# Twelve of the 72 weight pieces rounded between the blocks of the experts

## The chip, the cores and the metric

The kernel runs on one core of one Trainium2 chip. The metric is the device time of one execution in microseconds (us). The kernel before has three timed runs: 1114.82, 1117.33 and 1116.95 us, so a median of 1116.95 us.

## The reference, cut to what matters

```python
def _attn_ref(q, k, v):                       # 4 batches, 12 heads, 448 tokens, 64 wide
    scores = scale * np.matmul(q, k.transpose(0, 1, 3, 2)) - np.log(S)
    return np.matmul(1.0 / (1.0 + np.exp(-scores)), v)

def _moe_ref(x, expert_emb, tau, w1, w2):     # 1792 tokens of 768; 8 experts, 1024 wide
    expert_idx = np.argmax(logits, axis=1)
    for e in range(E):
        mask = expert_idx == e
        h = np.maximum(x[mask] @ w1[e], 0.0)
        out[mask] = gate_w[mask, None] * (h @ w2[e])

def _moe2_ref(x, w_a, w_b, w_out):            # 768 -> 1536 -> 768, weights in float64
    return ((x @ w_a) * (x @ w_b) @ w_out).astype(np.float32)
```

The three parts run one after the other: the attention's output is what the experts route, and their output is what the last part multiplies. `w_a`, `w_b` and `w_out` reach the kernel as float64, and no engine computes in that type.

## The kernel before, in words

**Pieces and units.** The last part's 1536 columns are cut into twelve steps `f` of 128. The weights of a step are three tiles (`w_a`, `w_b`, `w_out`) of 128 partitions by 768, and each tile is handled in two halves, so there are 72 units. `prep_load` (L171) fetches a unit's raw 64-bit words, 384 KB, into one of four `raw` buffers. `prep_unit` (L185) turns them into float32 with integer arithmetic: two instructions on VectorE (L195, L197, into one of two or three buffers `m`), two on ScalarE (L199, and L201 into one of three buffers `ab`) and one addition on GpSimd (L202). `prep_finish` (L205) makes the last instruction on VectorE (L212), and with `behind=1` leaves the newest unit for a later call, so that its addition has time. `prep_store` (L221) writes the result to a scratch tensor `wm` in DRAM. `prep_tick` (L226) is one round of all four, for one unit: store what is finished, finish what is added, fetch the unit three further on, start the next one.

**When units are done before.** `F_EARLY = 4` puts the 24 units of steps 0 to 3 into the attention, one `prep_tick` for each pair of heads and three extra ones. Their results pass through `wm`. The other 48 units belong to the last part's first group of rows.

**The experts.** The tokens of each half of the batches are sorted by expert into blocks of 128, and `block1` (L852) does one block `b`: transpose and split the next block's tokens, two halves of the first product (`p1`, 18 matmuls each), a transpose of the hidden rows (`h_tr`, split into `hTh` and `hTl`), the second product (`p2`, 48 matmuls), the scaling by the gate on VectorE (`y`), and a scatter of `y` by GpSimd. All matmuls work on float32 numbers split into a high and a low half: ScalarE makes the high half (L728), VectorE subtracts it to get the low one (L729). Where the next block has another expert, the new `w1` (six tiles, 1024 wide) and `w2` (eight, 768 wide) are split inside `tc.If` blocks: `w1` while the second product runs, `w2` around the start of the next block. Such a block is called a changing block below. The first 14 blocks (`LIVE`) always run, later ones only if they hold tokens. `tick()` inside a block pumps the routing work that is left and issues none of the rounding.

**The last part.** Rows are taken in four groups (512, 512, 512 and 256 rows), each of twelve steps. Step `i` splits the weights of step `i+1` (`w_split`), multiplies (`ab`: 36 matmuls on PE into two PSUM buffers; ScalarE copies the first half out, L1040, VectorE multiplies the second by it, L1043), transposes rows of the next group in steps 4 to 11 (`y_tr`, L724), and adds the step before into the output (`out_mm`, 24 matmuls). From step 4 on, `y_tr` sits between the two PSUM buffers, so the next step's first matmul takes the buffer that L1043 has to release. In the first group, `prep_more` does rounding units between these pieces, four in an even step and five in an odd one, as far as step `i+5`. Units of a step in this group are written straight into the buffer that `w_split` reads, and `w_split` calls `prep_tick` itself where the six units it needs are not yet finished. `w_load` (L982) fetches a step's weights from `wm` where they were not rounded in place. Every transfer named here is issued in program order by SP's one queue; every engine also works in program order.

Of the kernel before, what the change touches and what calls it, by code (L numbers as in the profile page):

```python
# [24 lines left out]
def build(ctx: ExitStack, tc: tile.TileContext, q, k, v, emb, tau, w1, w2, wa, wb, wo, out, dbg=None, stop=None):  # L25
# [27 lines left out]
    LIVE = LIVE0 + -(-CAP[1] // P)  # L53
# [107 lines left out]

    HU = DM // 2
    units = [(f, part, hf) for f in range(NF) for part in range(3) for hf in range(2)]
    F_EARLY = 4
    next_unit, unit_end = [0], [6 * F_EARLY]
    prep_raw = {}

# [53 lines left out]
    def prep_store(dma=nc.sync):  # L221
        while prep_out:
            o, t = prep_out.pop(0)
            dma.dma_start(out=o, in_=t)

    def prep_tick(dma=nc.sync, behind=0):  # L226
        prep_store(dma)
        prep_finish(behind)
        prep_load(next_unit[0] + 3, dma)
        prep_unit()  # L230
# [507 lines left out]
    def load_w(which, expert, pair):  # L738
        t, src = (r1[pair], w1) if which == 1 else (r2[0][:, 2 * pair:2 * pair + 2, :], w2)
        nc.sync.dma_start(out=t, in_=src[expert, 2 * pair * P:2 * (pair + 1) * P, :].rearrange("(k p) c -> p k c", p=P))  # L740

    def split_w(which, kk, pool=None):
        hi, lo = (w1h, w1l) if which == 1 else (w2_t["h"], w2_t["l"])
        t = r1[kk // 2][:, kk % 2, :] if which == 1 else r2[0][:, kk, :]
        split(hi[kk], lo[kk], t, hi[kk].bitcast(F32))
# [97 lines left out]
    def moe(r2_p):  # L843
        pool = moe_pool
        w2h, w2l, hTh, hTl = w2_t["h"], w2_t["l"], hT["h"], hT["l"]
        mx_p = pool("mx", 2)
        r2.append(r2_p.tile([P, KF, DM], F32, name="r2"))
        ps_1 = pool("ps_1", 2, space=PSUM)
        ps_2 = pool("ps_2", 2, space=PSUM)
        ps_x = pool("ps_x", 4, space=PSUM)  # L850
        misc["ps"] = lambda: ps_x.tile([P, 512], F32, tag="px", name="px")
        def block1(b, chg, was_new, load, e_load):  # L852
            def when_new(fn, chg=chg):
                if chg is not None:
                    with tc.If(chg == 1):
                        fn()

            def load_new(which):
                for i in range((KD if which == 1 else KF) // 2):
                    load_w(which, e_load, i)  # L860

            def split_new(which, k0, k1):
                for kk in range(k0, k1):
                    split_w(which, kk)

            def p1(hf, inner):
                p1_half(b, hf, ps_1.tile([P, FH], F32, tag="p1", name="p1"),
                        mx_p.tile([P, FH], F32, tag="h", name="h"), inner)

            def p2(yp, k0, k1):  # L870
                for kk in range(k0, k1):
                    for l, wv in ((hTh, w2h), (hTh, w2l), (hTl, w2h)):
                        for hf in range(2):
                            nc.tensor.matmul(yp[hf][:, :HD], lhsT=l[:, kk, :], rhs=wv[kk][:, hf * HD:(hf + 1) * HD],  # L874
                                             start=kk == 0 and wv is w2h and l is hTh,
                                             stop=kk == KF - 1 and l is hTl)

            def tick():
                if b < LIVE:
                    pump()  # L880
                    pump()

            if b > 0:
                when_new(lambda: load_new(1), load)
                p1(0, lambda: None)
                when_new(lambda: split_new(2, KF // 2, KF - 2), was_new)
                tick()

                def rest():
                    h_tr(b, 0)  # L890
                    when_new(lambda: split_new(2, KF - 2, KF), was_new)

                p1(1, rest)
                tick()
                when_new(lambda: load_new(2), load)
            yp = [ps_2.tile([P, 512], F32, tag="p2", name="p2") for _ in range(2)]
            p2(yp, 0, 1)
            h_tr(b, 1)
            p2(yp, 1, 2)
            x_load(b + 1)  # L900
            if b == 0:
                split_new(2, 4, KF)
                when_new(lambda: load_new(1), load)
                when_new(lambda: load_new(2), load)
            when_new(lambda: split_new(1, 0, KD))
            p2(yp, 2, KF // 2)
            gather(b + 2)
            tick()
            p2(yp, KF // 2, KF)
            tick()  # L910
            y = mx_p.tile([P, DM], F32, tag="y", name="y", bufs=1)
            for hf in range(2):
                nc.vector.tensor_scalar(out=y[:, hf * HD:(hf + 1) * HD], in0=yp[hf][:, :HD],
                                        scalar1=slots[:, 2, b:b + 1], scalar2=None, op0=ALU.mult)
            when_new(lambda: split_new(2, 0, KF // 2))
            ph = 0 if b < LIVE0 else 1
            j = b - TB[ph][0]

            nc.gpsimd.indirect_dma_start(out=ys_d if b < LIVE else ys_d[:Y0, :], out_offset=bass.IndirectOffsetOnAxis(ap=idy[ph][:, j:j + 1], axis=0),
                                         in_=y, in_offset=None)  # L920

        for i in range(2, KF // 2):
            load_w(2, e_of[0], i)

        def block(b, was_new=None):
            nx = b + 1
            if nx < NBLK:
                if b + 2 >= LIVE0:
                    while bg:
                        pump()  # L930
                chg = value(nx, 1, 1, [ET.Activation, ET.DVE, ET.Pool])
                load = value(b + 2, 3, 1, [ET.SP])
                e_load = value(b + 2, 4, E - 1, [ET.SP])
                live = value(nx, 0, 1, ENGINES) if nx >= LIVE else None
            else:
                chg = load = e_load = None
            block1(b, chg, was_new, load, e_load)
            if nx == LIVE:
                first_loads()
            if nx < LIVE:  # L940
                block(nx, chg)
            elif nx < NBLK:
                with tc.If(live == 1):
                    block(nx, chg)

        block(0)
        moe_s.close()


    def glu():  # L950
# [31 lines left out]
        def w_load(i):  # L982

            if i < len(steps):
                t = w_raw(i)
                if F_EARLY <= i < NF:
                    wraw[i] = [(s, slice(0, DM), t[:, s, :]) for s in range(3)]
# [7 lines left out]
        def w_split(i, parts=range(3), eng=nc.vector):  # L995
            if i < len(steps):
                if parts[0] == 0:
                    wsp[i] = [ws_p.tile([P, 3, DM], F32R, tag=nm, name=nm) for nm in ("whi", "wlo")]
                while F_EARLY <= i < NF and wr_n.get(i, 0) < 6:
                    prep_tick()  # L1000
# [170 lines left out]
```

## Time and profile before

| | |
|---|---|
| timed runs, median | 1116.95 us |
| the profiled execution | 1113.61 us, its span 1111.9 us |
| PE busy | 1070.6 us (96%) |
| VectorE busy | 603.3 us (54%) |
| ScalarE busy | 500.3 us (45%) |
| GpSimd busy | 178.2 us (16%) |
| DMA | 182.98 MB, mean 165 GB/s |
| 20th to 28th of 40 slices, PE in tenths | 9 9 7 9 8 8 8 9 8 |

The span runs through attention (up to about 205 us), the experts (up to about 546 us) and the last part. PE is busy in nearly every slice, and the slices that are below 9 lie in the change from attention to the experts, at the end of the experts and in the first group of the last part. A share over the whole span says little here, since the three parts have different limits; the rows below are therefore of single stretches. Times in rows are from the span's start.

### The profile page before, as it was taken

The page shows a single profiled execution, that of the slowest core. Times are in us where ns is not written, and L with a number is a line of the kernel's source. Part 1 is how long each engine was busy: PE and PEld are TensorE (multiplying, and loading weights), DVE is VectorE, ACT ScalarE, POOL GpSimd, SP SyncE. Part 2 cuts the span into 40 slices and gives each one's busy share as a digit, 9 for nine tenths or more (in the row PEclk, how much of TensorE's full clock was granted, in tenths as well). Part 3 has the DMA queues.
Part 4 walks back from the last instruction along what each step waited for, and adds up shares of the span by engine and source line. Part 5 has one row for each costly group of instructions (what it writes and reads, how often), then busy time and mean ns, then how long its engine had stood idle before and what let it go on. Part 6 is the DMA issues. An engine that isn't in the chain of part 4 may idle for free.

```text
span 1111.9 us, 16742 instructions
## 1 busy us (share of the span) xinstructions
PE 1070.6 (96%) x5996; PEld 870.6 (78%) x5996; DVE 603.3 (54%) x1037; ACT 500.3 (45%) x761; POOL 178.2 (16%) x218
## 2 busy tenths in 40 slices
PE   7999999999999999999798889899999999999998
PEld 4555555599989898989787677788888888888997
DVE  2556688864853585352287998643333343333553
ACT  5766767431743474431355556333323232223442
POOL 2121322231221222121123343200000000000000
PEclk9999999999999999999899999999999999999999
DMA  9478586436644775331368566545231072220730
GB/s 201 138 199 214 150 231 197 165 106 266 230 185 169 270 263 192 136 136 45 106 216 278 173 211 214 198 155 214 91 122 43 4 295 103 110 86 1 310 131 29
DMA packets 108681, 182.98 MB, mean 165 GB/s; under 512 B 49560, under 2 KB 80792, under 8 KB 102560
## 3 DMA queue, kind: packets, MB, share of 16 engines
q1 hardware_dynamic: 104608, 166.54, 44.7%
q0 software_dynamic: 3040, 14.94, 3.8%
q8 instruction: 49, 0.80, 0.3%
q14 instruction: 56, 0.46, 0.1%
q10 hardware_dynamic: 928, 0.23, 0.1%
HBM read 149.45 MB, written 32.24 MB: 163 GB/s over the span
## 4 chain that ended last, share of the span: by engine, by line
PE 36%; DVE 9%; DMA 3%; issue 2%; ACT 1%; POOLq 0%; POOL 0%; SPq 0%; ACTq 0%; DVEq 0%
PE ab L1035 8%; PE ab L1037 8%; PE ab L1036 8%; PE o L1068 4%; PE o L1069 4%; PE o L1070 4%; DVE wlo L729 3%; DVE m L195 2%; DVE m L197 1%; DVE wx L212 1%; DMA r<-wm 1%; DMA yg<-ys 1%; DVE r L212 1%; DVE m L1043 1%; DVE gl L729 0%
## 5 line engine op out<-in xcount | busy, mean ns | idle before, releaser
L1035 PE MATMUL ab<-yh,whi 128*128 128x512 f32 (+1 forms) x576 | 211.8, 368 | 17.1 <-DVE m L1043 13.8
L1036 PE MATMUL ab<-yl,whi 128*128 128x512 f32 (+1 forms) x576 | 210.7, 366 | 0.0
L1037 PE MATMUL ab<-yh,wlo 128*128 128x512 f32 (+1 forms) x576 | 210.4, 365 | 0.0
L1035 PEld LDWEIGHTS ab<-yh,whi 128*128 128x128 f32 x576 | 109.7, 190 | 35.2 <-DVE m L1043 15.3
L1037 PEld LDWEIGHTS ab<-yh,wlo 128*128 128x128 f32 x576 | 109.7, 190 | 17.7 <-DVE wlo L729 0.2
L1036 PEld LDWEIGHTS ab<-yl,whi 128*128 128x128 f32 x576 | 109.6, 190 | 16.0
L202 POOL TENSOR_TENSOR m<-m,raw 128x384 int32<-128x384 int32 x72 | 81.8, 1136 | 240.9 <-DVE m L197 77.8
L1068 PE MATMUL o<-whi,gh 128*128 128x512 f32 x336 | 114.7, 341 | 0.0
L1069 PE MATMUL o<-whi,gl 128*128 128x512 f32 x336 | 113.8, 339 | 0.0
L1070 PE MATMUL o<-wlo,gh 128*128 128x512 f32 x336 | 112.9, 336 | 0.0
L536 ACT ACTIVATE a<-ps,bias_s 112x896 f32<-112x896 f32 x96 | 91.6, 1005 | 30.6 <-PE ps L535 30.2
L728 ACT CAST gh<-m 128x512 fp32r<-128x512 f32 (+1 forms) x48 | 27.2, 567 | 169.5 <-DVE m L1043 169.5
L1043 DVE TENSOR_TENSOR m<-ab,a 128x512 f32<-128x512 f32 (+1 forms) x48 | 29.9, 623 | 128.3 <-PE ab L1037 128.3
L729 DVE TENSOR_TENSOR wlo<-r,whi 128x768 fp32r<-128x768 f32 x70 | 65.7, 993 | 45.8 <-ACT whi L728 45.8
L729 DVE TENSOR_TENSOR wlo<-wx,whi 128x768 fp32r<-128x768 f32 x72 | 67.5, 992 | 42.5 <-ACT whi L728 42.5
L790 PE MATMUL p<-w1h,xl 128*128 128x512 f32 x216 | 85.3, 395 | 2.4 <-DVE xl L729 2.4
L788 PE MATMUL p<-w1h,xh 128*128 128x512 f32 x216 | 86.6, 401 | 0.1
L789 PE MATMUL p<-w1l,xh 128*128 128x512 f32 x216 | 84.6, 392 | 0.0
L547 PE MATMUL av<-a,v 112*64 112x448 f32 x384 | 82.5, 551 | 0.0
L874 PE MATMUL p<-w2h,hTh 128*128 128x384 f32 x288 | 76.3, 345 | 0.0
L791 ACT ACTIVATE h<-p 128x512 f32<-128x512 f32 x34 | 20.4, 599 | 123.8 <-PE p L790 123.8
L728 ACT CAST whi<-wx 128x768 fp32r<-128x768 f32 x72 | 55.6, 832 | 42.1 <-PE o L1069 30.2
(224 smaller groups left out, 1894.5 us busy)
## 6 DMA issues: line engine op xcount, KB each, us to landing
wx<-wm SPq DMA_DIRECT2D x20, 1152.0 KB, 9.4
r<-wm SPq DMA_DIRECT2D x19, 1152.0 KB, 6.0
r<-in_moe_w_dram SPq DMA_DIRECT2D x28, 768.0 KB, 8.6
r<-in_moe_w_dram SPq DMA_DIRECT2D x18, 1024.0 KB, 6.3
raw<-in_moe_w_a_dram SPq DMA_DIRECT2D x24, 384.0 KB, 3.4
raw<-in_moe_w_b_dram SPq DMA_DIRECT2D x24, 384.0 KB, 3.5
raw<-in_moe_w_out_dram SPq DMA_DIRECT2D x24, 384.0 KB, 5.4
q<-in_q_dram SPq DMA_DIRECT2D x48, 112.0 KB, 4.3
```

Of the source, the lines that this page charges most:

```text
L536: nc.scalar.activation(out=a[:, c2], in_=ps[:, :, :S], func=AF.Sigmoid, bias=bias_s[:CP], scale=qscale)
L728: nc.scalar.copy(out=hi, in_=src)
L729: eng.tensor_tensor(out=lo, in0=src, in1=f32_hi, op=ALU.subtract)
L788: nc.tensor.matmul(ps, lhsT=xh[:, kk, :], rhs=w1h[kk][:, cs], start=kk == 0, stop=False)
L789: nc.tensor.matmul(ps, lhsT=xh[:, kk, :], rhs=w1l[kk][:, cs], start=False, stop=False)
L790: nc.tensor.matmul(ps, lhsT=xl[:, kk, :], rhs=w1h[kk][:, cs], start=False, stop=kk == KD - 1)
L1035: nc.tensor.matmul(ps[:, :n], lhsT=hi[:, s, cs], rhs=yh[:, kk, :n], start=kk == 0, stop=False)
L1036: nc.tensor.matmul(ps[:, :n], lhsT=hi[:, s, cs], rhs=yl[:, kk, :n], start=False, stop=False)
L1037: nc.tensor.matmul(ps[:, :n], lhsT=lo[:, s, cs], rhs=yh[:, kk, :n], start=False, stop=kk == KD - 1)
L1068: nc.tensor.matmul(t[:, d0:d1], lhsT=gh[:, cs], rhs=hi[:, 2, d0:d1], start=first, stop=False)
L1069: nc.tensor.matmul(t[:, d0:d1], lhsT=gl[:, cs], rhs=hi[:, 2, d0:d1], start=False, stop=False)
L1070: nc.tensor.matmul(t[:, d0:d1], lhsT=gh[:, cs], rhs=lo[:, 2, d0:d1], start=False, stop=last)
```

## The change

```diff
-    F_EARLY = 4
+    F_EARLY = 6
...
             p2(yp, 2, KF // 2)
             gather(b + 2)
             tick()
+            if 0 < b < LIVE - 1:
+                prep_tick(behind=1)
             p2(yp, KF // 2, KF)
             tick()
```

`F_EARLY = 6` makes the units of steps 4 and 5 early ones too. The attention still has 24 ticks, so it fetches three units more and rounds as many as before. Blocks 1 to 12 of the experts each round one unit, and 36 are left for the first group. The weights of steps 4 and 5 now pass through `wm`, so `w_load` fetches them in the first group.

VectorE in block 3, a changing block; `w1l` and `w2l` are the low halves of the new expert's weights, `y` the scaled output. Before:

```order
L729 TENSOR_TENSOR w1l_131<-r_2_2717,w1h_125 128x1024
L855 UNCONDITIONAL_BRANCH x3
L913 TENSOR_SCALAR y<-p_3646,slots 128x384
L913 TENSOR_SCALAR y<-p_3647,slots 128x384
L855 COMPARE_AND_BRANCH
L729 TENSOR_TENSOR w2l_2708<-r_2831,w2h_2700 128x768
```

And now:

```order
L729 TENSOR_TENSOR w1l_131<-r_2_2723,w1h_125 128x1024
L855 UNCONDITIONAL_BRANCH x3
L212 SCALAR_TENSOR_TENSOR ab<-ab,m 128x384
L195 TENSOR_SCALAR m<-raw 128x384
L197 SCALAR_TENSOR_TENSOR m<-raw,m 128x384
L915 TENSOR_SCALAR y<-p_3672,slots 128x384
L915 TENSOR_SCALAR y<-p_3673,slots 128x384
L855 COMPARE_AND_BRANCH
L729 TENSOR_TENSOR w2l_2714<-r_2837,w2h_2706 128x768
```

Three instructions of two units now stand between the split of `w1` and the scaling.

VectorE in the first group, from the end of step 6's multiplication into step 7, with the split for step 8 (`wlo`). Before:

```order
L212 SCALAR_TENSOR_TENSOR r_2831<-ab,m 128x384
L195 TENSOR_SCALAR m<-raw 128x384
L197 SCALAR_TENSOR_TENSOR m<-raw,m 128x384
L212 SCALAR_TENSOR_TENSOR r_2831<-ab,m_8621 128x384
L212 SCALAR_TENSOR_TENSOR r_2831<-ab,m 128x384
L195 TENSOR_SCALAR m<-raw 128x384
L197 SCALAR_TENSOR_TENSOR m<-raw,m 128x384
L729 TENSOR_TENSOR wlo<-r_2831,whi 128x768 x3
```

And now:

```order
L212 SCALAR_TENSOR_TENSOR wx_8751<-ab,m 128x384
L195 TENSOR_SCALAR m_8753<-raw 128x384
L197 SCALAR_TENSOR_TENSOR m_8753<-raw,m_8753 128x384
L729 TENSOR_TENSOR wlo<-r_2837,whi 128x768 x3
L212 SCALAR_TENSOR_TENSOR wx_8751<-ab,m 128x384
```

The two finishes and the whole unit that `w_split` had to call for itself before the split are gone.

SP's queue in the same group, steps 1 to 3: `wm_72` is step 4's weights, `yg` the next group's rows. Before:

```order
L992 DMA wx_8620<-wm_71 128x2304
L182 DMA raw<-in_moe_w_out_dram 128x768
L224 DMA wm_72<-r_2831 128x2304
```

And now:

```order
L700 DMA yg<-ys 96x768
L700 DMA yg<-ys 32x768
L178 DMA raw<-in_moe_w_b_dram 128x3x256 x2
L994 DMA r_2837<-wm_72 128x2304
L182 DMA raw<-in_moe_w_out_dram 128x768
L224 DMA wm_74<-wx_8751 128x2304
```

The store of step 4's weights has become a fetch, and it stands behind the eight fetches of the next group's rows.

## Rows read from the trace of the kernel before

**Rows 1.** Windows: busy us and instructions of PE, PEld, DVE, ACT, POOL; clock, DMA share, GB/s.

```profile
300.00:350.00 50.00, 49.66 (x271) 45.19 (x272) 24.66 (x33) 20.06 (x31) 10.68 (x6) 1.00 0.61 230
600.00:650.00 50.00, 41.70 (x205) 34.05 (x203) 46.74 (x69) 28.54 (x53) 19.49 (x17) 1.00 0.58 195
750.00:800.00 50.00, 50.00 (x247) 42.13 (x247) 17.26 (x22) 14.82 (x22) 0.00 (x0) 1.00 0.43 171
```

**Rows 2.** Waits of PE, 555 to 713 us: total us, times, longest.

```profile
PE ab L1035 <- DVE m L1043: 13.8, 6, 4.4
```

**Rows 3.** Timeline, VectorE, first group: start, us, instruction; steps 0 and 3 to 8.

```profile
564.68 0.69 DVE L1043 TENSOR_TENSOR m<-ab,a 128x512 f32<-128x512 f32 x1
...
609.16 0.68 DVE L1043 TENSOR_TENSOR m<-ab,a 128x512 f32<-128x512 f32 x1
...
621.58 0.68 DVE L1043 TENSOR_TENSOR m<-ab,a 128x512 f32<-128x512 f32 x1
...
636.49 0.69 DVE L1043 TENSOR_TENSOR m<-ab,a 128x512 f32<-128x512 f32 x1
...
649.39 0.68 DVE L1043 TENSOR_TENSOR m<-ab,a 128x512 f32<-128x512 f32 x1
...
666.75 0.69 DVE L1043 TENSOR_TENSOR m<-ab,a 128x512 f32<-128x512 f32 x1
...
681.99 0.68 DVE L1043 TENSOR_TENSOR m<-ab,a 128x512 f32<-128x512 f32 x1
```

**Rows 4.** Timeline, PE, step 10: its first matmul, and the transpose behind it.

```profile
700.10 0.50 PE L1035 MATMUL ab<-yh,whi 128*128 128x512 f32 x1 [3.12 <-DVE m L1043]
...
708.73 0.45 PE L724 MATMUL ab<-ident_r,yg 128*128 128x128 f32 x3 [0.18 <-ACT a L1040]
```

**Rows 5.** Timeline, ScalarE, first group: the split of step 3's weights.

```profile
586.12 2.31 ACT L728 CAST whi<-wx 128x768 fp32r<-128x768 f32 x3 [3.29 <-DMA wx<-wm]
```

**Rows 6.** Timeline, VectorE: a unit in the attention; L195 beside an addition.

```profile
172.67 0.55 DVE L212 SCALAR_TENSOR_TENSOR ab<-ab,m 128x384 f32<-128x384 f32 x1
173.14 0.35 DVE L195 TENSOR_SCALAR m<-raw 128x384 int32<-128x384 int32 x1
173.53 0.56 DVE L197 SCALAR_TENSOR_TENSOR m<-raw,m 128x384 int32<-128x384 int32 x1
174.00 1.08 DVE L522 TENSOR_TENSOR qkl<-pt,qkh 128x896 fp32r<-128x896 f32 x1
175.01 1.42 DVE L729 TENSOR_TENSOR w1l<-r,w1h 128x1024 fp32r<-128x1024 f32 x1
...
612.94 1.19 DVE L195 TENSOR_SCALAR m<-raw 128x384 int32<-128x384 int32 x1
```

**Rows 7.** Timeline, GpSimd: the addition of the unit in rows 6.

```profile
174.32 1.02 POOL L202 TENSOR_TENSOR m<-m,raw 128x384 int32<-128x384 int32 x1 [10.45 <-DMA xs<-xtok]
```

**Rows 8.** Timeline, VectorE, experts: blocks 3, 5 and 13.

```profile
285.54 6.91 DVE L729 TENSOR_TENSOR w1l<-r,w1h 128x1024 fp32r<-128x1024 f32 x6 [0.31 <-ACT w1h L728]
292.36 1.14 DVE L913 TENSOR_SCALAR y<-p,slots 128x384 f32<-128x384 f32 x2
...
298.62 0.69 DVE L729 TENSOR_TENSOR hTl<-px,hTh 128x512 fp32r<-128x512 f32 x1
...
326.92 1.14 DVE L913 TENSOR_SCALAR y<-p,slots 128x384 f32<-128x384 f32 x2 [4.86 <-PE p L874]
...
467.64 6.90 DVE L729 TENSOR_TENSOR w1l<-r,w1h 128x1024 fp32r<-128x1024 f32 x6 [0.30 <-ACT w1h L728]
...
478.99 0.55 DVE L212 SCALAR_TENSOR_TENSOR ab<-ab,m 128x384 f32<-128x384 f32 x1
```

**Rows 9.** Timeline, PE, experts: `h_tr` behind block 3; the matmul with `hTl` behind block 13.

```profile
300.14 0.66 PE L837 MATMUL px<-ident,h 128*128 128x128 f32 x4 [0.16 <-ACT h L791]
...
481.94 0.62 PE L874 MATMUL p<-w2h,hTl 128*128 128x384 f32 x2 [0.22 <-DVE hTl L729]
```

**Rows 10.** The tile `wm`, who waited for it (us, times): ScalarE for a buffer `ab`.

```profile
  ACT ab L201: 6.8, 2
```

## The prediction

> **What bounds the kernel now.** I read windows of the three parts first. While the experts run, PE is busy for 49.66 of 50 us, so only work that makes PE wait costs anything there; from the second group of the last part on it is busy for 50.00 of 50 with 247 instructions; in the first group it is busy for 41.70 with 205, while VectorE is at 46.74 of 50 [rows 1]. So the first group is where time can be won. Then PE's waits in that group: L1035, the first matmul of a half step, waits for VectorE's L1043 six times, 13.8 us in all [rows 2]. Then the timeline of L1043 on VectorE, whose starts are m(i), i being the step: m(3) to m(8) lie 12.42, 14.91, 12.90, 17.36 and 15.24 us apart [rows 3]. A step of PE is 63 instructions, and at 247 per 50 us it would take 12.75 [rows 1]. The fourth and fifth distances stand out because they hold 6 and 5 units and not 5 and 4: there `w_split` had to finish a unit by itself.
>
> **The first group.** From the three clean distances: 14.91 - 12.90 gives 2.01 us for a unit, 12.90 - 12.42 gives 0.48 for the transposed rows' low half, and 12.42 - 4 x 2.01 leaves 4.4 for the rest (L1043, its split, three `wlo`) [rows 3]. The order of the changed kernel has 3, 4, 5, 4, 5, 4, 5, 4 and 2 units between the L1043 of neighbouring steps, from step 0 on. PE's first step is untouched, so m(0) stays at 564.68. The first distance has three units but only one L212 of 0.47, so 4.4 + 6.0 - 0.9 = 9.5: m(1) at 574.2. The next four are 12.4, 14.4, 12.4 and 14.9, plus what the fetches of steps 3, 4 and 5 add.
>
> For those: the split of step 3's weights made ScalarE wait for their landing for 3.29 us [rows 5], because SP issues the fetch only behind the raw fetches of the units before it. Steps 4 and 5 were rounded in place and had no such wait. Now both have the fetch, and step 4's stands behind the eight fetches of `yg`. The three waits cost VectorE between nothing (two units of 2.01 stand ahead of each split and may cover them) and 3 x 3.29 = 9.9 us. I take the middle, 5, as 1, 3 and 1, with the 3 for step 4's fetch: m(2) at 587.6, m(3) 605.0, m(4) 618.4, m(5) 633.3. Before, m(4) was 621.58 [rows 3].
>
> From there no split has to call a unit, since all 36 are begun by the end of step 8. The distances are 12.9, 14.9, 12.9: m(6) 646.2, m(7) 661.1, m(8) 674.0, where it was 681.99. Behind m(8) VectorE has two units, 4.4 + 0.5 + 4.0 = 8.9, less than PE's step, and PE is the bound: its step 9 starts its multiplication when L1043's 0.68 are over, at 674.7, and step 10 12.75 later, at 687.5. From that start to the transposes of step 10 it was 708.73 - 700.10 = 8.63, which included 0.18 of waiting [rows 4]. They come at 696.1, not 708.73: **12.6 us gained**. With the other ends of the fetch waits it is 17.6 or 7.7. From these transposes to the end PE has no wait now, so nothing eats the gain.
>
> **The experts.** Each of blocks 1 to 12 gets a tick between the split of `w1` and `y`. In a block whose expert stays, VectorE waits 4.86 us for PE at `y` [rows 8], and the three instructions hide in that wait. In a changing block there is no such wait: from 285.54, where the split of `w1` begins, over `y` at 292.36 to `hTl` at 298.62, VectorE has no idle time at all, and it does not get ahead of PE [rows 8]. Six blocks show this, the first row at 285.54 and the last at 467.64 [rows 8]; the last is block 13, which gets no tick, so five pay.
>
> The price of one: L212, L195 and L197 take 174.00 - 172.67 = 1.33 us of VectorE [rows 6]. Then comes the addition on GpSimd. In the attention the same order occurs: L197, then an instruction that reads PSUM (L522, 1.08 us, about as long as the two `y`), then a `w1l`. The addition ran from 174.32 to 175.34 beside L522, and only the `w1l` behind it was longer, 1.42 [rows 6, 7] against 6.91 / 6 = 1.15 from start to start in a row of six [rows 8]; of that 0.2 is the wait for the addition, since a single one of the six ends some 0.07 after the next begins. So 1.53. The slack in front of PE: in block 13 one L212 of a drained unit already sits between two `w2l` [rows 8], 0.47 long, and PE waited 0.22 for `hTl` there [rows 9], so 0.25 is free; PE then also saves the 0.16 that `h_tr` waits for ScalarE [rows 9]. So 1.53 - 0.41 = 1.1 for each, 5.6 for five, and block 13, which now finishes two units instead of one, pays 0.47 more: **6.1 us lost**. Bounds: without the 0.2, 5.1. If an addition holds up both an L195, which takes 1.19 beside one instead of 0.35 [rows 6], and a `w2l`, and nothing is free, 5 x (1.33 + 2 x 0.84) + 0.47 = 15.5, more than the gain; I stay with 6.1, since the order of rows 6 is the very order here.
>
> The Trainium skill (page "SBUF — State Buffer", section "SBUF: two separate sides") says that VectorE and GpSimd share a port pair as an exclusive lock, which a VectorE instruction with two SBUF inputs and a GpSimd instruction take from each other for a whole instruction. By that rule alone a whole addition could stand ahead of the first `w2l`: the 0.84 of a blocked instruction in place of 0.2, which is the second rival below. The trace agrees with the lock (1.19 against 0.35) and with PSUM readers being spared [rows 6, 7].
>
> **The rest.** ScalarE's two instructions in a changing block stand ahead of its `w2h`, which VectorE reaches later still, so `w2l` hides them. The attention fetches three units more, 1.2 MB, at its end, where SP has finished its fetches of `q`, `k` and `v`; I take 0. Twelve stores and twelve fetches go between those of the experts' weights; a unit is fetched three ticks ahead, so I take 0 here too; if that cover went, a late raw piece would hold VectorE ahead of `y`.
>
> **Sum.** 6.1 - 12.6 = -6.5 us. Against the profiled execution's 1113.61 this is 1107.1. The median of the runs is 1116.95, 3.3 above that execution, so on that scale 1110.5.
>
> **Rivals.**
> 1. The two new fetches are late. All 9.9 us are paid: gain 7.7, loss 6.1, -1.6, so 1115.3. For it: SP spends its time on `yg` first. Against: with no units in step 0, the transfers ahead of it leave earlier.
> 2. The addition holds the first `w2l` for its whole length: 5 x (0.84 - 0.2) = 3.2 more, so 1113.7. For it: L195 shows the size [rows 6]. Against: rows 7, where a PSUM reader covered it.
> 3. Slower: ScalarE stops. L201 takes one of three `ab` buffers, and with `behind=1` the buffer's last store leaves SP in the very tick that needs it, behind the block's weight fetches. ScalarE would wait for that store ahead of `w2h`, and with it `w2l`, `hTl` and PE. The wait exists: 6.8 us in two [rows 10], 3.4 each. Two of them in changing blocks already take 6.8, the whole 6.5; in all five it is 17.0 - 6.5 = +10.5, so 1127.4. Against: in most of these blocks SP reaches the store a block earlier, and only where the weights of the next change are being fetched is it held.
> 4. The gain is in full and the cost at its low end: 17.6 - 5.1 = -12.5, so 1104.4; the low tail of the forecast.
>
> **Chances.** The forecast with its range (1106 to 1113) 0.60, rival 1 0.17, rival 2 0.13, rival 3 0.10. A measurement of this kernel can tell about 0.2%, 2.2 us: faster means below 1114.7, slower above 1119.2. The forecast is nearly always faster, rival 2 in most cases, rival 1 in three of ten: 0.71. Within 0.2%: most of rival 1 and a little of the others, 0.16. Slower: rival 3, and rival 1 where the loss is larger too, 0.13. The range 1105.5 to 1117.5 leaves out rival 3 and the tails.
>
> **What would show it.** In the profile after: ticks in blocks 3, 4, 7, 9 and 10 with `hTl` some 1.5 us later behind `y`'s old place and PE waiting for it 0.9 to 1.3 us each time; no wait in the others. In the first group, no two L212 in a row ahead of a `wlo`, distances of L1043 near 14.9 and 12.9 up to step 8, and PE's waits for L1043 at about half of the 13.8. Waits of ScalarE's `whi` for step 4's or step 5's weights above 5 us would make it rival 1; waits of L201 for `wm` in the experts, rival 3. The prediction is wrong in its ground if PE does not wait in the changing blocks, or if its waits in the first group stay.

## The result, and the profile after

| | before | after |
|---|---|---|
| time, median of 5 runs each, same chip | 1116.32 us (1114.82 to 1117.33) | 1106.16 us (1105.07 to 1109.68) |
| ratio, 95% interval | | 0.9917 [0.9900, 0.9934] |
| profiled execution, and its span | 1113.61, 1111.9 us | 1105.31, 1103.6 us |
| from `y` of block 0 to the last part's long row of transposes (L724, x21) | 313.27 us | 319.67 us |
| from there to m(0) | 15.25 us | 12.94 us |
| from m(0) to the transposes of step 10 | 144.05 us | 131.54 us |
| from there to the end | 403.17 us | 403.33 us |

The kernel became faster by 0.8%: 9 us by the ratio, 10 by the medians, 8.3 by the two spans. The forecast was 6.5, and the time lies in the range, 0.7 us above its lower end of 1105.5. All lines of the kernel are two higher after the change (L1043 is L1045). The nine digits of PE in the table of before are those of its 18th to 26th slices; apart from the first and last slice, PE is below 9 only in the 20th, 22nd to 24th and 26th, so not where the attention ends. The first group shows the gain, the experts the price. First the windows that answer to [rows 1], in the same columns:

```profile
300.00:350.00 50.00, 47.72 (x262) 43.69 (x263) 30.68 (x44) 22.46 (x36) 9.50 (x9) 1.00 0.72 266
...
600.00:650.00 50.00, 44.75 (x213) 37.12 (x212) 44.69 (x67) 28.92 (x53) 17.50 (x15) 0.93 0.60 206
650.00:700.00 50.00, 47.91 (x234) 39.87 (x233) 40.95 (x61) 25.40 (x46) 14.65 (x12) 1.00 0.56 199
750.00:800.00 50.00, 50.00 (x248) 42.15 (x247) 17.25 (x22) 14.82 (x22) 0.00 (x0) 1.00 0.34 124
```

The window from 650 to 700 us was, before:

```profile
650.00:700.00 50.00, 40.78 (x191) 33.27 (x190) 44.59 (x70) 27.74 (x52) 20.53 (x18) 0.97 0.61 205
```

In the experts PE lost nine instructions in 50 us, in the two windows of the first group it won eight and 43, and behind the group nothing moved. PE's waits from 555 to 715 us, which answer to [rows 2]:

```profile
PE ab L724 <- ACT a L1042: 4.8, 1, 4.8
PE py L724 <- issue: 3.0, 1, 3.0
PE ab L1037 <- DVE m L1045: 2.6, 2, 2.1
```

The 13.8 us of waiting for VectorE's multiplication are down to 2.6; the prediction had named about half as its sign. For ScalarE's copy `a` PE waited 4.5 us in five waits before; now it is one wait of 4.8 us. The multiplications of steps 0, 2, 3, 4 and 8 on VectorE's timeline, as in [rows 3]:

```profile
568.73 0.69 DVE L1045 TENSOR_TENSOR m<-ab,a 128x512 f32<-128x512 f32 x1 [3.10 <-PE ab L1039]
...
591.24 0.68 DVE L1045 TENSOR_TENSOR m<-ab,a 128x512 f32<-128x512 f32 x1
609.53 0.68 DVE L1045 TENSOR_TENSOR m<-ab,a 128x512 f32<-128x512 f32 x1
622.67 0.68 DVE L1045 TENSOR_TENSOR m<-ab,a 128x512 f32<-128x512 f32 x1
...
678.57 0.68 DVE L1045 TENSOR_TENSOR m<-ab,a 128x512 f32<-128x512 f32 x1
```

m(0) now waits 3.10 us for PE. Before, two units stood ahead of it, and PE's last matmul for it and VectorE's last instruction of the units ended within 0.1 us of each other. The long distance is m(2) to m(3), 18.29 us. ScalarE's timeline says why: these are its splits of the weights of steps 3, 4 and 5, each behind a wait for the fetch, and only the first of them stood in [rows 5]:

```profile
584.27 2.31 ACT L728 CAST whi<-wx 128x768 fp32r<-128x768 f32 x3 [2.93 <-DMA wx<-wm]
...
600.38 2.30 ACT L728 CAST whi<-r 128x768 fp32r<-128x768 f32 x3 [4.44 <-DMA r<-wm]
...
615.70 2.30 ACT L728 CAST whi<-r 128x768 fp32r<-128x768 f32 x3 [3.00 <-DMA r<-wm]
```

VectorE's timeline in the experts, block 3 (the next expert is new) and block 5 (it stays), to be held against [rows 8]:

```profile
285.54 6.90 DVE L729 TENSOR_TENSOR w1l<-r,w1h 128x1024 fp32r<-128x1024 f32 x6 [0.30 <-ACT w1h L728]
292.36 0.55 DVE L212 SCALAR_TENSOR_TENSOR ab<-ab,m 128x384 f32<-128x384 f32 x1
292.95 0.36 DVE L195 TENSOR_SCALAR m<-raw 128x384 int32<-128x384 int32 x1
293.34 0.56 DVE L197 SCALAR_TENSOR_TENSOR m<-raw,m 128x384 int32<-128x384 int32 x1
293.82 1.14 DVE L915 TENSOR_SCALAR y<-p,slots 128x384 f32<-128x384 f32 x2
294.87 5.35 DVE L729 TENSOR_TENSOR w2l<-r,w2h 128x768 fp32r<-128x768 f32 x6
300.15 0.68 DVE L729 TENSOR_TENSOR hTl<-px,hTh 128x512 fp32r<-128x512 f32 x1
...
325.63 0.56 DVE L197 SCALAR_TENSOR_TENSOR m<-raw,m 128x384 int32<-128x384 int32 x1
329.29 1.14 DVE L915 TENSOR_SCALAR y<-p,slots 128x384 f32<-128x384 f32 x2 [3.11 <-PE p L874]
```

In block 3 the unit starts when `w1l` ends, and `y` and `hTl` are 1.46 and 1.53 us later than before; in block 5 `y` still waits 3.11 us for PE. PE's one large wait in the experts (236 to 540 us) is for that `hTl`, in the five changing blocks and in block 13:

```profile
PE p L874 <- DVE hTl L729: 7.5, 6, 1.4
```

### The profile page after: what moved, and what is told of

The parts are those of the page before. It is cut to its first block, busy times and chain, and to the rows that moved or that the text cites. A ratio compares the mean times of both kernels' runs of the same rounds, so it can differ in the third digit from the quotient of the medians.

```text
span 1103.6 us, 16652 instructions
## 1 busy us (share of the span) xinstructions
PE 1068.9 (97%) x5996; PEld 871.9 (79%) x5996; DVE 599.8 (54%) x1037; ACT 500.4 (45%) x761; POOL 154.5 (14%) x218
## 5 line engine op out<-in xcount | busy, mean ns | idle before, releaser
L1037 PEld LDWEIGHTS ab<-yh,whi 128*128 128x128 f32 x576 | 109.3, 190 | 19.4 <-DVE m L1045 3.5
L1039 PEld LDWEIGHTS ab<-yh,wlo 128*128 128x128 f32 x576 | 109.2, 190 | 17.4
L1038 PEld LDWEIGHTS ab<-yl,whi 128*128 128x128 f32 x576 | 109.2, 190 | 15.5
L202 POOL TENSOR_TENSOR m<-m,raw 128x384 int32<-128x384 int32 x72 | 78.6, 1092 | 288.3 <-DVE m L197 91.2
L1045 DVE TENSOR_TENSOR m<-ab,a 128x512 f32<-128x512 f32 (+1 forms) x48 | 29.9, 622 | 138.0 <-PE ab L1039 138.0
L874 PE MATMUL p<-w2h,hTl 128*128 128x384 f32 x288 | 74.1, 338 | 7.5 <-DVE hTl L729 7.5
L728 ACT CAST whi<-r 128x768 fp32r<-128x768 f32 x70 | 53.9, 832 | 47.7 <-PE o L1071 40.1
```

Source lines behind the costliest of these rows:

```text
L1037: nc.tensor.matmul(ps[:, :n], lhsT=hi[:, s, cs], rhs=yh[:, kk, :n], start=kk == 0, stop=False)
L1038: nc.tensor.matmul(ps[:, :n], lhsT=hi[:, s, cs], rhs=yl[:, kk, :n], start=False, stop=False)
L1039: nc.tensor.matmul(ps[:, :n], lhsT=lo[:, s, cs], rhs=yh[:, kk, :n], start=False, stop=kk == KD - 1)
```

## The experiments

Theory: the change is the sum of a cost on VectorE in five blocks and a gain on VectorE in the first group. Rivals: the fetches' waits, ScalarE's waits for `ab`, and, from the result, something at the start of the last part, where 2.3 us went that no term held. All profiles in one table, in us; "late" is the time from the long row of transposes to VectorE's first `yl`. The times come from several chips; each ratio is against runs of before on the same chip, so kernels are compared by ratios or, stretch by stretch, by the columns:

| | `y` of block 0 at | to the transposes | to m(0) | late | to step 10's transposes | to the end | time, median | ratio to before |
|---|---|---|---|---|---|---|---|---|
| before | 236.16 | 313.27 | 15.25 | 2.87 | 144.05 | 403.17 | 1116.32 | |
| before_again | 236.19 | 313.55 | 14.99 | 2.68 | 145.70 | 403.07 | 1115.23 (one run) | |
| after | 236.12 | 319.67 | 12.94 | 0.69 | 131.54 | 403.33 | 1106.16 | 0.9917 [0.9900, 0.9934] |
| after_again | 238.77 | 319.71 | 11.85 | 0.69 | 129.75 | 403.32 | 1104.90 | 0.9885 [0.9861, 0.9909] |
| ticks_alone | 239.81 | 319.90 | 14.30 | 0.69 | 145.48 | 403.11 | 1122.13 | 1.0054 [1.0036, 1.0072] |
| gain_alone | 239.40 | 313.34 | 14.26 | 2.74 | 130.04 | 403.36 | 1102.37 | 0.9880 [0.9858, 0.9902] |
| before_padded | 236.43 | 313.33 | 12.71 | 0.68 | 145.45 | 403.08 | 1114.40 | 0.9982 [0.9966, 0.9999] |
| before_pad8 | 236.04 | 313.38 | 12.98 | 0.69 | 145.34 | 403.06 | 1115.19 | 0.9993 [0.9980, 1.0006] |
| after_padded | 239.48 | 319.40 | 14.45 | 2.77 | 130.47 | 403.30 | 1109.18 | 0.9935 [0.9919, 0.9952] |
| early_fetch | 236.38 | 319.95 | 12.81 | 0.69 | 127.55 | 403.31 | 1101.74 | 0.9863 [0.9839, 0.9888] |
| quiet_blocks | 237.81 | 315.49 | 12.19 | 0.69 | 132.35 | 403.36 | 1101.90 | 0.9868 [0.9844, 0.9893] |
| quiet_spread | 236.86 | 314.64 | 12.16 | 0.68 | 132.26 | 403.88 | 1100.51 | 0.9841 [0.9816, 0.9866] |
| spread_early | 238.11 | 314.73 | 12.55 | 0.68 | 127.59 | 403.32 | 1098.01 | 0.9838 [0.9817, 0.9859] |
| seven_early | 239.39 | 329.04 | 12.36 | 0.69 | 126.54 | 403.47 | 1110.87 | 0.9950 [0.9933, 0.9966] |

The attention ends up to 3.7 us apart between kernels that do the same there, so a column is compared rather than a span.

**The two halves apart.** `ticks_alone` rounds the twelve pieces in the experts and again in the first group; `gain_alone` rounds them nowhere:

```
 ticks_alone (from after)
-    F_EARLY = 6;  unit_end = [6 * F_EARLY]
+    F_EARLY = 4;  unit_end = [36]
-        unit_end[0] = len(units)
+        next_unit[0], unit_end[0] = 24, len(units)
 gain_alone (from before)
-    F_EARLY = 4;  unit_end = [6 * F_EARLY]
+    F_EARLY = 6;  unit_end = [24]
-        unit_end[0] = len(units)
+        next_unit[0], unit_end[0] = 36, len(units)
-    nc.sync.dma_start(out=t, in_=wm_d[steps[i][1]])
+    f = steps[i][1]
+    nc.sync.dma_start(out=t, in_=wm_d[f - 2 if f in (4, 5) else f])
```

> The twelve pieces are rounded in the expert blocks as after the change, and their results are not used: the last part's first group rounds the same 48 pieces as before. So this is the cost of the experts alone. Theory A (the prediction's account): the blocks in which the next expert is new lose 1.1 to 1.25 us each by one piece's 1.5 us on VectorE, the others nothing, block 13 about 0.5 us; in all 6.1 to 6.4 us, and the time is 1116.3 + 6.4 = 1122.7 us, with m(0) of the first group 6 us later and all distances behind it as before. Rival: part of the changed kernel's cost or gain comes from how the group's start meets the transfers of the experts' end; then this kernel is not 6 us slower but, by the 2.3 us found at the start, only about 4 us (1120.4 us).

> The twelve pieces of steps 4 and 5 are not rounded anywhere (their steps fetch the weights of steps 2 and 3 instead, so the output is not the reference's): the attention and the experts do what they did before, the last part's first group what it does after the change. So this is the gain alone. Theory A (the prediction's account): the first group loses two rounding steps' worth, 12.5 us, and the experts change nothing; 1116.3 - 12.5 = 1103.8 us if the start of the group is as before, or 1101.5 us if the 2.3 us at its start belong to the group's new order of fetches. Rival (the cost of the experts lies with the twelve pieces' transfers and not with VectorE, so it partly stays): 1106 us or more.

Measured: 1122.13 and 1102.37 us. The experts' column of `ticks_alone` is 6.6 above the first profile of before, `gain_alone`'s differs by 0.1; the first group's is 14.0 below it in `gain_alone`, and in `ticks_alone` between those of the two profiles of before. So the two terms are where the prediction had them. Whether they are the whole, the times leave open: 1.0054 and 0.988 give 0.9933 together, about 7 us of gain, which lies at the end of the first interval of the change (0.9900 to 0.9934) and outside the second (0.9861 to 0.9909). The column to m(0) does show a rest: 14.30 and 14.26 us in the halves, 12.94 and 11.85 with both. The halves are late for different reasons. In `gain_alone` VectorE's `yl` is late, as before. In `ticks_alone` it is punctual, but VectorE waits for ScalarE's split of step 1's weights (which waits 2.68 us for their fetch), and two units still stand between this and m(0):

```profile
568.86 2.70 DVE L729 TENSOR_TENSOR wlo<-r,whi 128x768 fp32r<-128x768 f32 x3 [1.90 <-ACT whi L728]
```

**The start of the last part.** The first step was to see whether the 2.3 us stay.

> The kernel before, profiled a second time. The changed kernel gained about 2.3 us more at the start of the last part than the prediction's terms hold: from the first long row of transposes to m(0) 12.94 us against 15.25 us before, and before, VectorE's first yl began 2.85 us after ScalarE's first yh against 0.68 us after the change. Theory A (a property of the program before: something that the kernel's code or its transfers bring about each time): this profile again has about 15.2 us and 2.8 us. Theory B (chance of one execution): it has about 13 us and 0.7 us, and the kernel before is then some 2 us shorter in its span, near 1110 us.

> The changed kernel once more, as the measure for the others of this group. Theory: the start of its last part is a property of the program, so VectorE's first yl starts 0.7 us after the long row of transposes began (0.69 in the first profile, and 0.69 in both variants that round in the expert blocks; 2.87, 2.68 and 2.74 in the two profiles of before and in the variant that has before's experts), and the first m follows about 12.9 us after it; time 1106 us. Rival (chance): about 2.8 us and 14 to 15 us.

They do: `yl` is 2.68 us late again before, 0.69 again after. The timelines of before, then of after, ScalarE's and VectorE's first instruction of the last part:

```profile
549.45 1.86 ACT L728 CAST yh<-py 128x384 fp32r<-128x384 f32 x4 [10.24 <-DVEq L943]
...
552.30 1.95 DVE L729 TENSOR_TENSOR yl<-py,yh 128x384 fp32r<-128x384 f32 x4 [6.42 <-DMA r<-wm]
```

```profile
555.80 1.86 ACT L728 CAST yh<-py 128x384 fp32r<-128x384 f32 x4 [10.06 <-DVEq L945]
...
556.48 1.95 DVE L729 TENSOR_TENSOR yl<-py,yh 128x384 fp32r<-128x384 f32 x4 [4.07 <-ACT yh L728]
```

The `r<-wm` named as releaser before is only the last event ahead of 552.30: in both programs `yl` waits for expert weights that landed long ago, and after the change it starts 2.3 us ahead of the landing of that fetch (issued at 555.76, 3.0 us on its way). The trace places the delay more closely. VectorE leaves the nested `tc.If` blocks by a branch (L943, L945). Before, its next recorded instruction, the first semaphore check ahead of `yl`, comes 2.33 us behind the end of this branch; after the change, 0.16 us. In the four late profiles of the table it is 2.15 to 2.33 us, in the ten others 0.15 or 0.16.

On PE the delay is a wait ahead of the first matmul. Before, then after:

```profile
553.93 0.77 PE L1035 MATMUL ab<-yh,whi 128*128 128x512 f32 x1 [1.63 <-DVE yl L729]
```

```profile
558.46 0.76 PE L1037 MATMUL ab<-yh,whi 128*128 128x512 f32 x1
```

It is 1.4 to 1.9 us in the late profiles, and the punctual ones have none. That is not all of the 2.3 us. The window from the transposes to m(0), before and after, columns as in [rows 1]:

```profile
549.43:564.68 15.25, 13.62 (x59) 11.30 (x60) 11.62 (x21) 10.19 (x21) 1.02 (x1) 0.70 0.62 209
```

```profile
555.79:568.73 12.94, 12.94 (x59) 11.04 (x60) 9.15 (x16) 8.52 (x17) 0.00 (x0) 0.75 0.92 337
```

The same 59 matmuls and transposes of PE took 13.62 us at a granted clock of 0.70, 12.94 us at 0.75, and 11.85 us at 0.86 in `after_again` (13.54 at 0.70 in `before_again`): part of each window lies at the lower of the two levels, 1.2 GHz, behind a change of stage in which PE stood still for some 4 us. So 0.7 us of the 2.3, and 1.7 of the 3.1 between the second profiles, are the clock's. The clock does not follow the delay: it is 0.76 in `gain_alone`, which is late, and 0.75 in the punctual profile after the change.

What differs between late and punctual programs is how many VectorE instructions stand ahead of the last part in the program's text, paths not taken included: 2,123 before and in `gain_alone`, both late; 2,056 after and in `ticks_alone`, 2,079 in `quiet_blocks`, all punctual. So that number alone was shifted, by instructions on a tile of one column that compute nothing, in blocks where VectorE waits: 61 in before, then 8, and 67 in after, which brings it to 2,123.

```
+        pad = mx_p.tile([P, 1], F32, tag="pad", name="pad", bufs=1)
...
             gather(b + 2)
             tick()
+            for _ in range({1: 15, 2: 15, 5: 15, 6: 16}.get(b, 0)):   # before_pad8: {1: 8}
+                nc.vector.memset(pad, 0.0)                            # after_padded: 67, behind prep_tick
```

> The kernel before with 61 VectorE instructions on a tile of one column more, put into expert blocks 1, 2, 5 and 6 where VectorE waits for TensorE: they compute nothing that is used, and shift all of VectorE's later code by 61 instructions, so that the code of the last part begins at the same place of a piece of 8 KB of code (128 instructions of 64 bytes) as in the changed kernel. Theory A (VectorE's late start is the fetch of its own code: the late programs fetch two pieces of 8 KB just after the transposes begin, the punctual ones only one): yl starts about 0.7 us after the transposes, the first m 14.3 us after them instead of 15.0 to 15.25, and the rest is as before; about 1 us less, 1114.5 us. Theory B (it is the transfers of weights at that place, or the semaphores): yl still 2.7 to 2.9 us late and the time 1115.6 us.

> The kernel before with only 8 of the 61 VectorE instructions, in block 1: what is open is how finely the late start depends on the place of VectorE's code (2,123 VectorE instructions ahead of the last part: late, also in the changed kernel padded to that count; 2,056, 2,079, 2,082 and 2,184: punctual). Here there are 2,131. Theory A (an edge of the code lies within the first few instructions of the last part, and VectorE stops at it): 8 instructions move the edge ahead of the part, yl starts 0.7 us behind the transposes, 12.7 us to the first m, 1114.4 us as with 61. Theory B (it depends on a wide stretch of places, or on the distance from the edge): yl is still 2.7 to 2.9 us late, and the time that of the kernel before.

> The counterpart of the kernel before with 61 VectorE instructions put in: the changed kernel with 67 such instructions of one column (in the quiet blocks, ahead of y, while VectorE waits there), so that VectorE's code of the last part begins at the very instruction count at which it begins in the kernel before. Theory A (about 2 us of what the change gained came only from where VectorE's code of the last part falls): the late start comes back, yl starts 2.7 to 2.9 us after the long row of transposes instead of 0.7, the first m 14 to 15 us after them instead of 11.9 to 12.9, and the time is 1106.5 to 1107.5 us, some 2 us above the changed kernel's 1104.9. Theory B (the place of VectorE's code alone doesn't decide; the shift before worked by something else): yl stays at 0.7 us and the time at 1105 us.

The shift decides whether `yl` is late, in both directions. `before_padded`, then `after_padded`:

```profile
549.77 1.86 ACT L728 CAST yh<-py 128x384 fp32r<-128x384 f32 x4 [10.27 <-DVEq L946]
...
550.44 1.95 DVE L729 TENSOR_TENSOR yl<-py,yh 128x384 fp32r<-128x384 f32 x4 [4.25 <-ACT yh L728]
```

```profile
558.90 1.69 ACT L728 CAST yh<-py 128x384 fp32r<-128x384 f32 x4 [9.91 <-DVEq L948]
...
561.65 0.56 DVE L729 TENSOR_TENSOR yl<-py,yh 128x384 fp32r<-128x384 f32 x1 [5.99 <-DMA r<-wm]
```

Eight instructions are enough. The stretch to m(0) goes to 12.71 and 12.98 us, shorter than the 14.3 expected for 61 (that number was `ticks_alone`'s, which has the wait for step 1's weights), and back to 14.45 in `after_padded`. In time the gain of before is small: 0.9982 [0.9966, 0.9999] with 61 instructions, not told from nothing with 8. `after_padded` has 0.9935: without the lucky place of its code the change is worth 7 us (5 to 9). That is clear of the change's second measurement, 0.9885, but not of its first, 0.9917; what the place of the code is worth in time is therefore known only roughly (0.8 and 2.0 us in the two padded kernels of before, 2.0 and 5.6 us against the two measurements of the change). One part of the expectation fell: the pieces of code fetched by the instruction queue just behind the transposes were to be two where `yl` is late and one where it isn't. In a window of 1 us from the transposes, `before_padded` and `after_padded` have

```profile
q14 instruction: 2, 0.02, 5.6%
```

```profile
q14 instruction: 1, 0.01, 3.4%
```

so the punctual one has two, the late one has one. The five kernels whose experts are those of before have two in that window, the nine others one, late or not. That VectorE's place in the code makes it late is shown; by what step is open. The Trainium skill (page "Runtime: NRT & Kernel Launch", section "Instruction fetch mechanics") says that a branch to code outside the two pages held makes the engine fetch that page first. VectorE does come out of branches here, and an edge that 8 instructions move fits the rule; the counts of fetched pieces do not bear it out.

**The fetch waits.**

```
-            w_load(i + 2)
+            for n in {0: (2, 4), 1: (3, 5), 2: (), 3: ()}.get(i, (i + 2,)):
+                w_load(n)
```

> The changed kernel with the fetches of the weights of steps 4 and 5 issued two steps earlier, in steps 0 and 1, as soon as their tiles are free. It tells how much of ScalarE's waits for fetched weights in steps 3, 4 and 5 (2.93, 4.44 and 3.00 us) counts. Theory A (the prediction's sum took 5 us of such waits into the time): the waits of steps 4 and 5 go and the first group is 3 to 5 us shorter, 1101 to 1103 us. Rival B (the group is bound by VectorE and TensorE, and the waits are idle time of an engine that is ahead): no change, 1105.5 to 1107 us. Rival C (the earlier fetches take the transfer engines from those of steps 2 and 3): the waits move to steps 2 and 3, and it is up to 3 us slower.

Theory A, at its low end: 1101.74 against `after_again`'s 1104.90 us on the same chip (the two intervals of the ratio still overlap), and 127.55 in the first group against 129.75 and 131.54. ScalarE's three splits have become

```profile
584.09 2.31 ACT L728 CAST whi<-wx 128x768 fp32r<-128x768 f32 x3 [2.34 <-DMA wx<-wm]
...
597.36 2.29 ACT L728 CAST whi<-r 128x768 fp32r<-128x768 f32 x3
...
609.76 2.29 ACT L728 CAST whi<-r 128x768 fp32r<-128x768 f32 x3
```

7.4 us of waits went, and 2 to 4 us of time: the rest of these waits had cost nothing. With the waits went a dip of TensorE's clock. The window from 610 to 630 us, columns as in [rows 1], of after and of `early_fetch`:

```profile
610.00:630.00 20.00, 14.96 (x64) 12.33 (x65) 16.94 (x28) 13.14 (x24) 7.41 (x7) 0.83 0.71 247
```

```profile
610.00:630.00 20.00, 18.90 (x94) 15.70 (x93) 19.11 (x29) 12.21 (x23) 7.65 (x6) 1.00 0.58 187
```

A granted 0.83 means part of the window at the lower of the two levels (1.2 GHz), in a window in which PE was busy for 14.96 of 20 us and had its wait of 4.8 us for ScalarE; with the fetches early, 18.90 busy, it stays at 2.4 GHz. The six profiles in which PE waits there for 3 to 5 us all have the dip; `early_fetch`, `spread_early` and `seven_early` have neither.

**The experts' cost, moved to where VectorE waits.**

```
 quiet_blocks
-            if 0 < b < LIVE - 1:
-                prep_tick(behind=1)
+            for _ in range(2 if b in (1, 2, 5, 6, 8, 11) else 0):
+                prep_tick(behind=1)
 quiet_spread: one prep_tick there, the other behind y's scatter
```

> As the change, but the twelve pieces lie two by two in blocks 1, 2, 5, 6, 8 and 11, in which no new expert's first weights are split, and none in the others. Theory A (the cost is VectorE's length in the blocks that are bound by VectorE; a quiet block has an idle stretch of 3.1 us ahead of y, in which two pieces of 1.5 us fit): the experts cost 0 to 1 us instead of 6.4, and the time is 1106.2 - 6 = 1100 us (1099 to 1101.5). Rival (the cost is the pieces' own, by their transfers or by GpSimd's addition beside VectorE, wherever they lie): 1105 to 1108 us, with quiet blocks longer than 18.0 us.

> As the variant with two pieces in each of blocks 1, 2, 5, 6, 8 and 11, but the second piece stands behind y and its scatter instead of directly behind the first. There ScalarE waited 9.5 us (block 6) for the store that frees a tile ab, this store stood in SyncE's queue behind a load that waited for GpSimd, and block 6 took 19.4 us instead of 18.0 and block 2 0.65 us more. Theory A (that is the third rival of the prediction, a wait of ScalarE for the store of ab, brought on by two pieces at once): the waits of ScalarE for these stores shrink below what delays the next block, block 6 takes 18.0 us, and the experts cost 0.5 to 1 us instead of 2.2; time 1100 us. Rival (the cost in blocks 2 and 6 is the length of two pieces on VectorE): as before, 2 us of cost, 1102 us.

The changing blocks were back at 18.4 us from `hTl` to `hTl`, as before the change (19.6 with it), so the cost is VectorE's length there. But the quiet blocks, which split no new `w1`, did not take the pairs for nothing: the experts cost 2.2 us, not 0 to 1. In block 6 of `quiet_blocks` the timeline has

```profile
347.15 1.14 DVE L915 TENSOR_SCALAR y<-p,slots 128x384 f32<-128x384 f32 x2 [0.93 <-PE p L874]
349.43 0.34 SPq L224 DMA_DIRECT2D wm<-ab  x1
351.89 0.55 ACT L201 ACTIVATE ab<-raw 128x384 f32<-128x384 bf16 x1 [9.54 <-DMA wm<-ab]
...
353.37 0.55 ACT L201 ACTIVATE ab<-raw 128x384 f32<-128x384 bf16 x1 [0.49 <-DMA wm<-ab]
...
354.67 0.60 ACT L791 ACTIVATE h<-p 128x512 f32<-128x512 f32 x1 [0.75 <-ACTq L855]
```

L201 needs a tile `ab` whose store leaves SP late; `h`, for which PE waits next, stands behind it. This is rival 3 of the prediction, in other blocks than it named. Spread out, the waits of L201 still sum to 31 us, as against 34, but block 6 takes 18.7 us instead of 19.4, and the cost is 1.1 to 1.4. Time 1100.51, as expected; the waits did not shrink much, against the expectation; they mostly stopped holding up `h`.

**Both together, and one step more.** `spread_early` is `quiet_spread` with the earlier fetches. `seven_early` adds step 6: `F_EARLY = 7`, two units in blocks 5, 8 and 11 and three in 1, 2, 6 and 12.

> The two variants that were faster than the change, together: one piece ahead of y and one behind it in blocks 1, 2, 5, 6, 8 and 11, and the fetches of steps 4 and 5 two steps earlier. If their causes are apart (experts' length by VectorE; fetches that ScalarE waits for in the first group), the gains add: from the changed kernel's 1104.9 us, 4.4 us and 3.2 us less, 1097.3 us, with m(0) to m(8) about 106 us (105.85 with the early fetches, 109.16 without them). If both took away the same wait, about 1100 us.

> As the one before, but step 6's six pieces are also rounded early: eighteen pieces in the experts, two in each of blocks 5, 8 and 11 and three in each of 1, 2, 6 and 12, none in the blocks with a new expert's weights, and 30 in the first group. Theory A (each step of rounding taken out of the first group is worth 6.2 us there, and quiet blocks have the room, as VectorE is idle 7 us behind y): 6 us less than with twelve pieces, 1091 to 1093 us. Rival (ScalarE's waits for the stores of ab, and SyncE's queue behind them, now decide the quiet blocks; 31 us of such waits stand in the variant with twelve, and it lost 0.7 us in block 6): the blocks with three lose 1 to 2 us each, and the time is 1095 to 1099 us.

`spread_early`, 1098.01 us, has the lowest median of all. Its columns are those of its two parents (314.73 and 127.59), so the causes are apart; its ratio can't be told from `quiet_spread`'s. It chooses blocks by this input's experts, so it is a probe rather than a rule. `seven_early` missed both expectations. Its first group is only 1.05 us shorter, not 6: in `spread_early` m(0) to m(8) had already come down to 13.2 us a step, and PE's own step is 12.7. And the experts took 15.5 to 15.8 us longer than in the two profiles of before. The timeline of block 2:

```profile
275.15 0.35 SPq L224 DMA_DIRECT2D wm<-ab  x1
...
282.54 0.54 ACT L201 ACTIVATE ab<-raw 128x384 f32<-128x384 bf16 x1 [13.89 <-DMA wm<-ab]
...
288.36 0.60 ACT L791 ACTIVATE h<-p 128x512 f32<-128x512 f32 x1
...
289.01 1.11 PE L837 MATMUL px<-ident,h 128*128 128x128 f32 x4 [6.76 <-ACTq L855]
```

Three L201 wait in turn, `h` stands behind them, and PE waits 6.76 us; in block 6 it waits 3.88 in the same way. While PE waits, its clock falls: from 286.9 to 293.7 us the granted clock is 0.50, the level of 1.2 GHz, so some of the 15 us are the clock's. Rival 3 is real: nothing with one unit a block, 1 to 2 us with two in six blocks, 15 with three in four and two in three.

## Why the prediction was right, point by point

- **Changing blocks, 1.1 us each and 0.47 in block 13, 6.1 in all.** Right: 6.40 and 6.16 in the two pairs of profiles, five periods of `hTl` longer by 1.15 to 1.24, block 13 by 0.46, PE's waits 7.5 in six. The parts were split otherwise: the unit took 1.46 to `y` instead of 1.33, and the addition held `w2l` by 0.06 (5.35 against 5.29) instead of 0.2. So rival 2 is out; beside the addition stands `y`, which reads PSUM, as in [rows 6, 7]. One reading there is loose: L195, the 1.19 against 0.35, has a single input in SBUF, so it shows that the addition holds VectorE up, but not the case of two inputs for which the prediction gave the rule.
- **First group, 12.6 us from m(0) on.** 12.5 in the first pair of profiles, 16.0 in the second (129.75 against 145.70). The pairs differ because `before_again` has one dip of the clock more behind m(8), and because the three waits for fetches were shorter in `after_again`, 7.8 us against 10.4. m(8) was forecast 109.3 us behind m(0) and came at 109.84.
- **The fetch waits, taken as 5 of 0 to 9.9.** The waits of ScalarE were 10.4 us, above the bound, and the two that `early_fetch` took away were worth 2 to 4 us; step 3's stayed there, and its worth is open. The bound went wrong because it took step 3's 3.29 for all three; step 4's was 4.44. Rival 1 needed all 9.9 to count; of the 7.4 us that went, 2 to 4 did.
- **"PE's first step is untouched, so m(0) stays at 564.68".** This is the step that failed, by 2.3 us, and 3.1 in the second pair. The change moved VectorE's code, and with it went PE's wait for `yl`, 1.63 and 1.45 us; the rest, 0.7 and 1.7, is TensorE's clock in this stretch, which no experiment set. That two units ahead of m(0) went as well, which the prediction passed over, made no difference: in `before_padded`, which has them, m(0) waits 0.42 us for PE. With the code moved back, 0.9935 is -7.2 us, against the forecast's -6.5.
- **Rival 3** did not come: L201 waited in the experts, 17.4 us in five waits (4.3 of them named after the stores of `ab`; 14.6 and 9.5 in the second profile), but the changing blocks with such a wait grew by no more than the others. It came as soon as units were closer.
- **Rival 4**, 1104.4 us, is near the measured time, but neither of its conditions came true: the gain from m(0) on was 12.5 and not 17.6 us, the cost 6.4 and not 5.1.
- **Scale.** The forecast added the 3.3 us that the median of before lay above its profiled execution. After, it lies 0.9 above. Part of the 4.3 us between forecast and median is only that. It was also luck that the time stayed in the range: the terms alone put it near the middle, the 2.3 us that no term held and this scale carried it to 0.7 us above the lower end, and the second measurement, 1104.90, lies below it.

## What to carry to other kernels

Side work placed in a stage costs what it adds to the engine that is the bound there, and nothing in a block where this engine waits: price it by block, and then look at what the placed work itself waits for (a tile whose store stands in another engine's queue), since that decides how densely it may stand. Work taken out of a stage is worth its length only until the next engine's own length is reached; here the first two steps gave some 6 us each and the third 1. Before a difference of 0.2% is put down to the change that was made, shift an engine's code by a few idle instructions and see whether it stays.

## What the hardware showed that was not expected

Eight VectorE instructions of 0.06 us, placed 300 us earlier, changed when VectorE starts the last part by 2 us (2.87 and 2.68 to 0.69), and 67 of them brought the delay back (2.77) in the other kernel. The instructions that VectorE waits for there and the program's transfers were left as they were; the 2 us lie between a branch of VectorE and the first instruction recorded behind it.
